# A list scheduler's table of step times, latencies and priorities, replaced as a whole, in a one-core attention, gated-FFN and cosine-FFN kernel

## The chip, the cores and the metric

The kernel runs on 1 core of one Trainium2 chip. The metric is the device time of the program in microseconds (us). The granted clock of TensorE was 0.999 of full speed over the profiled execution.

## The reference

All tensors are fp32. Attention over 4 batches × 8 heads, 576 tokens, head size 64, then two feed-forward layers over 2304 tokens × 512:

```python
scores = q @ k.T / sqrt(64)
scores = where(scores >= max(scores) - tau, scores, -1e9)
attn = exp(scores - max(scores)); attn /= sum(attn) + 1e-09
x = attn @ v                                  # 2304 x 512 over all heads
xn = x / sqrt(mean(x * x) + 1e-06) * rms_g
x = (silu(xn @ w_gate) * (xn @ w_val)) @ w_out   # 512 -> 1536 -> 512
h = x @ w_in                                  # 512 -> 2048
out = (h * cos(h)) @ w_out2                   # 2048 -> 512
```

## The kernel before

**Arithmetic.** A fp32 product is made of three matmuls on a high and a low part of each operand (`mm3`, L829 to L831; every `po`, `pc`, `px`, `pgv` of the layers is issued at L831). Both layers replace 8 block products by 7 (Strassen's way): products are called p1 to p7 and issued as p1, p2, p6, p5, p7, p4, p3. p1, p6, p7 and p4 follow each other in one PSUM bank, so between two of them an ACT copy of the bank (`rc` L1434 in layer 1, `rc2` L1721 in layer 2) or a DVE add must have read it. Weights arrive as 64-bit values and are converted on the chip (L398 to L416 during attention, L1061 to L1075 and others later).

**Stages**, in the time of the profiled execution: a head without much work on TensorE (0 to 8 us); attention to 283 us, 16 pairs of heads × 5 units of up to 128 queries × 2 heads; an early part of layer 1 (`pgv`, `px`; 283 to 331 us); the 7-product part of layer 1 (to about 722 us); layer 2, overlapped with the end of layer 1 from about 700 us on (to 1087.6 us); a tail of one add and the last output transfer.

**Attention.** A unit does scores `s` (L597), row maximum (L618, DVE), `exp` (L637, ACT), mask and row sum (L647, DVE), transposes `pst` on TensorE (L687) through a ring of three PSUM banks that ACT empties (`et<-pst`, L697), a remainder `psc` (L706 to L711, emptied by L715), and the product with v, `po` (L724: `av0`, `av1`), in one PSUM bank that ACT empties (`t<-po`, L734). Per pair the division (`div`, L741), squares (`sq`, L751) and their sum (`x_add`, L755) run on POOL; per batch a sum by matmuls with ones (`pss`, L764) and the root (L769, L775).

**What sets the order.** The kernel is written as steps. Each kind of step has a row in the table `STEPS`: its engine, its assumed time in ns, an offset to its place, and sometimes a landing time of its own (else that of its engine in `SIGNAL`). `Plan.order` (L208) simulates these times: again and again it takes the step that can start earliest, among equals the one of the smallest place, and puts it out. So the table decides the order of instructions on every engine, and nothing else of the program: the hardware waits on data at run time, whatever times the table holds. Steps of the kinds in `LOCK` share one simulated port of DVE and POOL, and a POOL step of the kinds in `BEHIND` gets a real dependence on the last such DVE step that was put out before it.

```python
        eng, ns, place, landing = (STEPS[kind] + (SIGNAL[STEPS[kind][0]],))[:4]
...
                    if best is None or (t, s["place"], n) < best:
                        best = t, s["place"], n
```

The place of a step is the offset plus 3500 (`UNIT`) times the unit of work that the program puts it at.

Of the kernel before, what the change touches and what calls it, by code (L numbers as in the profile page):

```python
# [25 lines left out]

UNIT = 3500
STEPS = {
    "xl3": ("SP", 2500, -17237051, 4000),
    "yl": ("SP", 3000, 1818983, 3000),  # L30
    "oc0": ("ACT", 620, -178776),
    "none": ("", 0, -8569405),
    "load_k": ("SP", 1700, -7132505, 5000),
    "load_q": ("SP", 2300, -18780962, 7000),
    "load_v": ("SP", 1700, 8049624, 5000),
    "pb": ("PE", 440, -91272),
    "pa": ("PE", 440, -8753194),
    "pc": ("PE", 355, 18191),
    "pb_a": ("ACT", 477, 288563),
    "pa_a": ("ACT", 580, 5964477),  # L40
    "pc_a": ("ACT", 362, -19061587),
    "pa_l": ("DVE", 605, -7927289),
    "pb_l": ("DVE", 605, -17590911),
    "pc_l": ("DVE", 470, -10454287),
    "s": ("PE", 885, -18879084),
    "s4": ("PE", 790, 9187294),
    "warm": ("PE", 640, 5100),
    "max": ("DVE", 680, -18861462),
    "exp": ("ACT", 675, 7067125),
    "th": ("POOL", 300, 3913872),  # L50
    "mask": ("DVE", 742, -235624),
    "t": ("PE", 445, 43347),
    "raw": ("ACT", 477, -526274),
    "c0": ("PE", 245, -944825),
    "c1": ("PE", 465, -9009928),
    "c_raw": ("ACT", 295, 1709382),
    "radd": ("POOL", 250, 4551371),
    "rinv": ("DVE", 375, 1620120),
    "r_out": ("SP", 2100, 9184652, 2500),
    "r_in": ("SP", 1700, 1717211, 11000),  # L60
    "av0": ("PE", 2212, -17630008),
    "av1": ("PE", 2745, -11610484),
    "avo": ("ACT", 300, 1749559),
    "div": ("POOL", 1385, 2473400),
    "xout": ("SP", 800, -8632135, 2500),
    "sq": ("POOL", 1122, 5175409),
    "x_add": ("POOL", 1385, 7064993),
    "xsum": ("PE", 1085, 828449),
    "mean": ("DVE", 140, -17859185),
    "rms": ("POOL", 1520, 12341),  # L70
    "rs_out": ("SP", 2500, -17590004, 2500),
    "x_load": ("SP", 600, -18407685, 4500),
    "x_p": ("POOL", 1010, 6936870),
    "x_a": ("ACT", 540, -160662),
    "x_d": ("DVE", 480, 5142752),
    "jdma": ("SP", 500, -587219, 5000),
    "j1": ("DVE", 440, 914524),
    "j2": ("DVE", 608, -18600102),
    "j_p": ("POOL", 1310, 11607829),
    "j_a": ("ACT", 540, -8610871),  # L80
    "gv": ("PE", 2090, 467903),
    "silu": ("ACT", 420, -17284285),
    "px": ("PE", 2090, -18876387),
    "pxc": ("ACT", 400, -7101975),
    "hmul": ("DVE", 480, -18857593),
    "hhi": ("ACT", 420, 1874630),
    "hlo": ("DVE", 480, -18400468),
    "gv_": ("PE", 2090, 1352763),
    "silu_": ("ACT", 420, -18407990),
    "px_": ("PE", 2090, 1742320),  # L90
    "pxc_": ("ACT", 400, 9160368),
    "hmul_": ("DVE", 480, 1821227),
    "hhi_": ("ACT", 420, -11626266),
    "hlo_": ("DVE", 480, -223025),
    "x_q": ("DVE", 480, -19287661),
    "x_a_": ("ACT", 540, 456116),
    "x_d_": ("DVE", 480, 2080948),
    "ld": ("SP", 1700, -16315, 2600),
    "st": ("SP", 1350, 994979, 2300),
    "re": ("SP", 1350, -18655029, 2300),  # L100
    "wj1": ("DVE", 420, 1306287),
    "wj2": ("DVE", 640, -18827972),
    "wm": ("ACT", 650, 7535685),
    "wp": ("POOL", 1310, 6985902),
    "ws": ("POOL", 720, -179615),
    "whi": ("ACT", 590, -38166),
    "wlo": ("DVE", 640, -19073380),
    "vhi": ("ACT", 370, 720),
    "vlo": ("DVE", 370, -9649757),
    "ty": ("DVE", 1700, 5179345),  # L110
    "tz": ("DVE", 480, 2119290),
    "tp": ("DVE", 880, -7385897),
    "thi": ("ACT", 830, 1707682),
    "tlo": ("DVE", 880, -186196),
    "tr": ("POOL", 1010, 779397),
    "tg": ("ACT", 480, 6985043),
    "pr": ("PE", 1050, 1271768),
    "p1": ("PE", 1050, 2576303),
    "rc": ("ACT", 470, 264284),
    "ra": ("DVE", 530, 3761292),  # L120
    "rs": ("ACT", 470, 43510),
    "rm": ("DVE", 500, -19406559),
    "rh": ("ACT", 480, 3025557),
    "rl": ("POOL", 1010, -18138630),
    "po": ("DVE", 900, 8219776),
    "pq": ("ACT", 800, 3470758),
    "wt": ("DVE", 350, 1371338),
    "ld2": ("SP", 1700, 4594862, 2600),
    "st2": ("SP", 1350, -151407, 2300),
    "re2": ("SP", 1350, 1749849, 2300),  # L130
    "wj12": ("DVE", 420, 1947299),
    "wj22": ("DVE", 640, -100554),
    "wm2": ("ACT", 650, 368993),
    "wp2": ("POOL", 1310, 7156916),
    "ws2": ("POOL", 720, 2588453),
    "whi2": ("ACT", 590, 287276),
    "wlo2": ("DVE", 640, 449005),
    "vhi2": ("ACT", 370, 984685),
    "vlo2": ("DVE", 370, 1294887),
    "tz2": ("DVE", 480, 2726933),  # L140
    "tp2": ("DVE", 880, -277554),
    "thi2": ("ACT", 830, -7727467),
    "tlo2": ("DVE", 880, 286304),
    "pr2": ("PE", 1050, 4791879),
    "oo": ("PE", 1390, 4793082),
    "tlp2": ("POOL", 1950, 2138257),
    "rc2": ("ACT", 470, -10651785),
    "ra2": ("DVE", 550, 2274412),
    "ct": ("ACT", 600, 2047040),
    "cf": ("DVE", 550, -18746959),  # L150
    "df": ("DVE", 530, 932632),
    "cb": ("ACT", 520, 4959718),
    "cs": ("ACT", 620, 1869941),
    "cg": ("DVE", 550, -7077025),
    "dg": ("DVE", 530, -11626296),
    "gh": ("ACT", 500, -179772),
    "gl": ("POOL", 1020, 2435746),
    "oe": ("DVE", 690, 5135108),
    "oc": ("ACT", 620, 1804210),
    "so": ("SP", 500, 4701633, 3000),  # L160
}
SIGNAL = {"PE": 190, "DVE": 110, "ACT": 145, "POOL": 60, "SP": 100, "": 0}
SWITCH = 100

LOCK = {
# [22 lines left out]
class Plan:  # L188
# [8 lines left out]
    def add(self, kind, at, fn, *args, after=(), take=(), free=()):  # L197
        eng, ns, place, landing = (STEPS[kind] + (SIGNAL[STEPS[kind][0]],))[:4]
        step = {
            "n": len(self.steps), "kind": kind, "at": at, "place": place + at * UNIT, "eng": eng, "ns": ns, "landing": landing,  # L200
            "fn": lambda: fn(*args), "after": [x for x in after if x], "take": take, "free": free,
        }
        for key in free:
            self.users[key] = self.users.get(key, 0) + 1
        self.steps.append(step)
        return step
# [87 lines left out]
def attention_moe_cos_kernel(  # L294
# [164 lines left out]
    nat, qk, un, hf, pr, xb, rm, sq, pre = {}, {}, {}, {}, {}, {}, {}, {}, {}  # L459
# [563 lines left out]
    def moe(plan, gm, g3, gvs, x1, x2_, x3, y3, pxc3):  # L1023

        add = plan.add
# [3 lines left out]
        def at(us):  # L1029
            return LATER + us / 3.5  # L1030
# [20 lines left out]
        raw, tmp, wd, lds = {}, {}, {}, []  # L1051
# [88 lines left out]
        for m, (g, prs) in enumerate(PASS):  # L1140
            fresh = m <= FIRST or not g
            save = m < FIRST
            for j in range(2):
                i = groups[g][1][j]
                t = due(m, j) - 26
                if fresh:
# [9 lines left out]
                    def op(o, a, b, fn):  # L1156
                        return lambda eng=pool if m else vec: eng.tensor_tensor(o(), a(), b(), op=fn)

                    def part(fn, a, b):
                        return lambda: fn(a, b)  # L1160

                    after = {tag: order[tag] and [] or [] for tag in order}
# [4 lines left out]
                    ws = "ws" if m else "wt"  # L1167
# [3 lines left out]
                    s4 = add(ws, at(t + 9), op(part(gate, 2, 4), part(gate, 2, 4), part(gate, 0, 2), SUB), after=[s2])  # L1171
# [4 lines left out]
                else:  # L1176
                    old, st = kept[g, j]
# [6 lines left out]
            for j in range(2):  # L1184
                i = groups[g][1][j]
                t = due(m, 1) + 12 + 3 * j - 24
# [6 lines left out]
                else:  # L1193
                    old, st = kept["out", g, j]
# [7 lines left out]
        y, z = {}, {}  # L1202
# [5 lines left out]
        def t_steps(pr):  # L1208

            c, c2 = pr  # L1210
            t = {0: -22, 2: 2, 4: BLOCK * first[pr] - 30}[c]
            ztag = "r" if not c else "hh"
            ttag = "ttb" if c == 2 else "tt"
            take = {cc: [("y", ("y", cc))] if cc != 5 else [] for cc in pr}
# [22 lines left out]
            ys = {}  # L1237
            for cc in pr:
# [4 lines left out]
                else:  # L1243
                    after = ys.get(c, [])[-1:] + XS[2, 3][1:]
# [9 lines left out]
            def z_sub(kk):  # L1254
                if not kk:
                    for n in range(2):
                        z[c, n] = late[ztag].tile([P, TC], F32, tag=ztag, name="z")
                vec.tensor_tensor(z[c, kk], y[c2][:, 2 + kk], y[c2][:, kk], op=SUB)

            zs = []  # L1260
            for kk in range(2):
                zs.append(add("tz", at(t + 1), lambda kk=kk: z_sub(kk), after=ys[c2] + zs, take=[(ztag, ("z", c, n)) for n in range(2)] if not kk else []))

            def psub(a, b, o):
                return lambda: vec.tensor_tensor(o(), a(), b(), op=SUB)
# [533 lines left out]
        t = t_l2  # L1799
# [315 lines left out]
```

## Time and profile before

| what | value |
|---|---|
| device time, 3 runs | 1095.17 us median (1093.99 to 1095.41) |
| the profiled execution: its own time / its span | 1093.68 us / 1091.9 us |
| instructions | 18813 |
| busy share PE, PE loads, DVE, ACT, POOL | 99%, 89%, 78%, 63%, 40% |
| chain that ended last | PE 96%, ACT 2%, DVE 1% |
| HBM | 139 GB/s over the span |

The span is the time on the core's engines in one profiled execution; the device time of that execution is 1.8 us longer. PE is the matmul part of TensorE and PEld its weight loads, which overlap. A bracket at a row's end is the engine's idle time before it and the instruction that ended it.

### The profile page before, as it was taken

Reading aid. Unit: us, or ns where it says so; the run is one execution under the profiler, and the core shown is the slowest. Engines: PE = TensorE matmul, PEld = TensorE weight load, DVE = VectorE, ACT = ScalarE, POOL = GpSimd, SP = SyncE. Lnnn points to the kernel's source line nnn. Section 1 sums busy time; section 2 is a strip of 40 time slices with the busy share of each in tenths; the row PEclk is TensorE's granted clock in tenths of the full one; section 3 lists DMA queues with packets and bytes.
Section 4 is the critical chain, followed back from the end, with each engine's and each line's share of the span. In section 5 each row is a group of like instructions: output and inputs, shape, how many; then the busy total and the mean of one; then the engine's idle time right before and its main releaser. Section 6 shows DMA issues by size and latency. Waiting matters only on the chain.

```text
span 1091.9 us, 18813 instructions
## 1 busy us (share of the span) xinstructions
PE 1079.7 (99%) x6720; PEld 975.5 (89%) x6720; DVE 854.0 (78%) x1683; ACT 692.5 (63%) x1316; POOL 432.5 (40%) x445
## 2 busy tenths in 40 slices
PE   8999999999999999999999999999999999999998
PEld 7777777777899999999999999988898889888887
DVE  7999999989689777586756653788888887865665
ACT  5888888888567554545545442587776666765553
POOL 1234244253532545655331441445455455222221
PEclk9999999999999999999999999999999999999999
DMA  5342443322635465643132576424544344274633
GB/s 133 90 132 80 117 121 99 102 67 60 190 98 204 153 214 192 198 171 110 59 95 80 167 264 225 165 70 143 184 176 153 131 169 145 53 256 145 195 104 97
DMA packets 113453, 152.97 MB, mean 140 GB/s; under 512 B 51632, under 2 KB 82128, under 8 KB 113360
## 3 DMA queue, kind: packets, MB, share of 16 engines
q1 hardware_dynamic: 112000, 151.31, 43.0%
q8 instruction: 53, 0.87, 0.4%
q10 hardware_dynamic: 1264, 0.43, 0.2%
q14 instruction: 40, 0.33, 0.1%
q0 software_dynamic: 96, 0.03, 0.0%
HBM read 103.16 MB, written 48.58 MB: 139 GB/s over the span
## 4 chain that ended last, share of the span: by engine, by line
PE 96%; ACT 2%; DVE 1%; DMA 0%; issue 0%; SPq 0%; ACTq 0%
PE pc L831 38%; PE po L831 18%; PE px L831 14%; PE po L724 8%; PE s L597 7%; PE pst L687 5%; PE pgv L831 3%; PE psc L706 1%; ACT et L697 1%; PE psa L518 0%; PE pss L764 0%; DMA k<-in_k_dram 0%; PE psb L518 0%; ACT e L637 0%; PE warm L796 0%
## 5 line engine op out<-in xcount | busy, mean ns | idle before, releaser
L831 PE MATMUL pc<-xh,w 128*128 128x384 f32 x896 | 257.1, 338 | 0.0
L831 PEld LDWEIGHTS pc<-xh,w 128*128 128x128 f32 x896 | 164.6, 188 | 2.2
L831 PE MATMUL pc<-xl,w 128*128 128x384 f32 x448 | 151.0, 337 | 0.0
L831 PE MATMUL pc<-th,w 128*128 128x384 f32 x448 | 132.8, 337 | 0.0
L1674 POOL TENSOR_TENSOR h<-hh,h 128x384 fp32r<-128x384 f32 x64 | 64.9, 1019 | 142.7 <-DVE hh L1657 48.7
L1075 POOL TENSOR_TENSOR wtmp<-wtmp,raw 128x512 int32<-128x512 int32 x68 | 89.2, 1320 | 75.5 <-DVE wtmp L1070 23.2
L1771 DVE TENSOR_TENSOR acc<-acc,po 128x512 f32<-128x512 f32 x126 | 85.1, 683 | 34.4 <-PE po L831 33.7
L1430 DVE TENSOR_TENSOR r<-r,pc 128x384 f32<-128x384 f32 x96 | 52.6, 550 | 74.6 <-ACT r L1434 54.5
L1434 ACT COPY r<-pc 128x384 f32<-128x384 f32 x96 | 45.9, 481 | 100.8 <-PE pc L831 100.5
L831 PE MATMUL po<-w,h 128*128 128x512 f32 x405 | 109.7, 396 | 0.0
L637 ACT ACTIVATE e<-s,m 128x576 f32<-128x576 f32 x128 | 95.9, 798 | 12.1 <-DVE s L618 11.9
L647 DVE SCALAR_TENSOR_TENSOR e<-s,th,e 128x576 f32<-128x576 f32 x128 | 102.2, 830 | 0.8 <-POOL th L628 0.7
L831 PE MATMUL px<-h,w 128*128 128x384 f32 x516 | 102.4, 338 | 0.0
L618 DVE TENSOR_SCALAR_CACHE_REDUCE s<-s 128x576 f32<-128x576 f32 x128 | 91.5, 752 | 5.8 <-PE s L597 5.5
L831 PEld LDWEIGHTS px<-h,w 128*128 128x128 f32 x516 | 91.7, 188 | 0.0
L831 PEld LDWEIGHTS po<-w,h 128*128 128x128 f32 x405 | 75.5, 188 | 14.0
L831 PEld LDWEIGHTS pc<-xl,w 128*128 128x128 f32 x448 | 84.2, 188 | 2.0
L1445 POOL TENSOR_TENSOR h<-q,h 128x384 fp32r<-128x384 f32 x43 | 44.2, 1033 | 101.9 <-DVE q L1473 40.1
L831 PEld LDWEIGHTS pc<-th,w 128*128 128x128 f32 x448 | 82.8, 188 | 1.7
L697 ACT COPY et<-pst 128x512 f32<-128x512 f32 x144 | 77.3, 604 | 8.3 <-PE pst L687 7.7
L831 PE MATMUL pc<-tl,w 128*128 128x384 f32 x224 | 75.6, 338 | 0.3 <-DVE tl L1572 0.3
L724 PE MATMUL po<-et,vn 128*64 128x320 f32 (+1 forms) x512 | 69.1, 412 | 1.4 <-ACT et L697 1.4
(194 smaller groups left out, 2653.6 us busy)
## 6 DMA issues: line engine op xcount, KB each, us to landing
wd<-w SPq DMA_DIRECT2D x67, 512.0 KB
w<-wd SPq DMA_DIRECT2D x53, 512.0 KB
raw<-in_moe_w_out_dram SPq DMA_DIRECT2D x30, 512.0 KB
raw<-in_moe_w_in_dram SPq DMA_DIRECT2D x16, 512.0 KB
raw<-in_moe_w_gate_dram SPq DMA_DIRECT2D x14, 512.0 KB
raw<-in_moe_w_val_dram SPq DMA_DIRECT2D x14, 512.0 KB
wq<-wd SPq DMA_DIRECT2D x14, 512.0 KB
x<-xb SPq DMA_DIRECT2D x16, 288.0 KB
```

The costliest lines, as they stand in the source:

```text
L597: nc.tensor.matmul(un[n]["ps", hd][:, c, 0:288], lhs, kh[bb][r, k0:k0 + 288], start=c not in [d for d, _ in todo[:x]], stop=c not in [d fo ...
L618: nc.vector.tensor_scalar(s.rearrange("p (c n) -> p c n", c=2), un[n].pop(("ps", hd))[:, :, 0:288], qscale[:, 0:1] if n % 5 == 4 else 1.0, ...
L637: nc.scalar.activation(un[n]["e"][:, hd], un[n]["s", hd], AF.Exp, bias=grp[group_of(n)]["m"][:, c], scale=-1.0)
L647: nc.vector.scalar_tensor_tensor(e, un[n].pop(("s", hd)), grp[group_of(n)]["th"][:, ci:ci + 1], e, op0=ALU.is_le, op1=ALU.mult, accum_out= ...
L687: nc.tensor.transpose(ps[:, c], e[:, hd, k0:k0 + P], ident)
L697: nc.scalar.copy(dst, src)
L724: nc.tensor.matmul(po[64 * hd:64 * hd + 64, :], vn[:, hd, c, :] if c < 4 else vl[:, hd, :], hf[j]["et"][:, hd, c, :] if c < 4 else hf[j][" ...
L831: nc.tensor.matmul(ps, w[a], x[bb], start=first and i == 0, stop=last and i == 2, skip_group_check=more)
L1075: pool.tensor_tensor(tmp[key], tmp[key], raw.pop(key)[:, :, :, 0], op=ADD)
L1430: return add("ra", at(t0 + when - 60), lambda: vec.tensor_tensor(tile_[o], tile_[o], ps[BANK[n]], op=ADD), after=after + [steps[n]], free= ...
L1674: hs2[x] = add("gl", at(t - 60), lambda: pool.tensor_tensor(H[x][1], g_tile[x], f(H[x][0]), op=SUB), after=[y], free=[("qq", x)])
L1771: vec.tensor_tensor(o, o, oacc.pop((c, q)), op=ADD)
```

## The change

All rows of `STEPS` get a new place offset, about 80 of them a new time and three (`rh`, `cs`, `gh`) a landing of their own; `SIGNAL` gets new latencies; and one kind of step, the subtraction `tz` (L1258) of the second and later pairs of blocks in layer 1, additionally waits for the first two steps `silu_`. No instruction is added or removed: each engine executes the same set as before (PE 6354, DVE 1397, ACT 1321, POOL 450, SP 577 rows in the program), in another order.

```diff
 STEPS = {
-    "oc0": ("ACT", 620, -178776),
+    "oc0": ("ACT", 482, 1004465),
...
-    "rc": ("ACT", 470, 264284),
+    "rc": ("ACT", 376, -10036888),
...
-SIGNAL = {"PE": 190, "DVE": 110, "ACT": 145, "POOL": 60, "SP": 100, "": 0}
+SIGNAL = {"PE": 200, "DVE": 114, "ACT": 138, "POOL": 55, "SP": 100, "": 0}
...
-                zs.append(add("tz", at(t + 1), lambda kk=kk: z_sub(kk), after=ys[c2] + zs, take=[(ztag, ("z", c, n)) for n in range(2)] if not kk else []))
+                zs.append(add("tz", at(t + 1), lambda kk=kk: z_sub(kk), after=ys[c2] + zs + ([s for s in plan.steps if s["kind"] == "silu_"][:2] if c else []), take=[(ztag, ("z", c, n)) for n in range(2)] if not kk else []))
```

The first 29 steps on PE and its last 8 stand as before. Three places show how the rest moves.

**Place 1: PE at the end of attention** (`pst` and `psc` are transposes, `po` with 64x256 is `av0` of the last unit pair, with 64x320 `av1`). Before:

```order
L687 MATMUL pst<-ident,e 128x128 x16
L724 MATMUL po<-et,vn 64x256 x8
L724 MATMUL po<-ec,v_101 64x256 x2
L706 MATMUL psc<-ident,e 128x128 x2
L710 MATMUL psc<-swap,el 128x128
L711 MATMUL psc<-ident,el 64x128
L687 MATMUL pst<-ident,el 128x128 x4
L724 MATMUL po<-et,vn 64x320 x8
L724 MATMUL po<-ec,v_101 64x320 x2
```

The change, on the same engine:

```order
L687 MATMUL pst<-ident,e 128x128 x12
L706 MATMUL psc<-ident,e 128x128 x2
L710 MATMUL psc<-swap,el 128x128
L711 MATMUL psc<-ident,el 64x128
L687 MATMUL pst<-ident,e 128x128 x4
L687 MATMUL pst<-ident,el 128x128 x4
L724 MATMUL po<-et,vn 64x256 x8
L724 MATMUL po<-ec,v_101 64x256 x2
L724 MATMUL po<-et,vn 64x320 x8
L724 MATMUL po<-ec,v_101 64x320 x2
```

The remainder and the last transposes now stand ahead of `av0`, and `av1` directly behind it.

**Place 2: PE in the early part of layer 1** (`pgv` is gate or value, `px` the product with w_out, `pss` the last sum of squares). Before, around `pss`:

```order
L831 MATMUL pgv<-xl,w 128x384
L831 MATMUL pgv<-xh,w 128x384 x2
L831 MATMUL pgv<-xl,w 128x384
L831 MATMUL pgv<-xh,w 128x384
L764 MATMUL pss<-ones,sq 128x1 x5
L831 MATMUL pgv<-xh,w 128x384
L831 MATMUL pgv<-xl,w 128x384
```

The change:

```order
L831 MATMUL pgv<-xl,w 128x384
L831 MATMUL pgv<-xh,w 128x384 x2
L831 MATMUL pgv<-xl,w 128x384
L831 MATMUL pgv<-xh,w 128x384
L764 MATMUL pss<-ones,sq 128x1 x5
L831 MATMUL px_4816<-hhi,w 128x384
L831 MATMUL px_4816<-hlo,w 128x384
L831 MATMUL px_4816<-hhi,w 128x384
```

`pss` moves from behind a `px` and a `pgv` group to ahead of that `px` group.

**Place 3: PE where layer 1 ends in layer 2** (`pc<-th,w` and the like are p7's last matmuls, `pc<-th,a` p4's first; six `po` with 128x512 are one output set of layer 2). Before:

```order
L831 MATMUL pc<-th,w 128x384
L831 MATMUL pc<-tl,w 128x384
L831 MATMUL pc<-th,w 128x384 x2
L831 MATMUL pc<-tl,w 128x384
L831 MATMUL pc<-th,w 128x384
L831 MATMUL pc<-th,a 128x384
L831 MATMUL pc<-tl,a 128x384
```

The change:

```order
L831 MATMUL pc<-th,w 128x384
L831 MATMUL pc<-tl,w 128x384
L831 MATMUL pc<-th,w 128x384 x2
L831 MATMUL pc<-tl,w 128x384
L831 MATMUL pc<-th,w 128x384
L831 MATMUL po<-w,h 128x512 x3
L831 MATMUL po<-w,hhi 128x512 x2
L831 MATMUL po<-w,hlo 128x512
L831 MATMUL pc<-th,a 128x384
L831 MATMUL pc<-tl,a 128x384
```

An output set now stands between p7 and p4.

## Rows read from the trace of the kernel before

**Rows 1.** The page, part 1: busy us (share of the span) xinstructions.

```profile
PE 1079.7 (99%) x6720; PEld 975.5 (89%) x6720; DVE 854.0 (78%) x1683; ACT 692.5 (63%) x1316; POOL 432.5 (40%) x445
```

**Rows 2.** The page, part 4: the chain that ended last, shares by engine.

```profile
PE 96%; ACT 2%; DVE 1%; DMA 0%; issue 0%; SPq 0%; ACTq 0%
```

**Rows 3.** Windows: stretch, us, busy us of PE, PEld, DVE, ACT, POOL, clock, DMA share, GB/s.

```profile
40.00:275.00 235.00, 234.11 (x2102) 179.02 (x2099) 224.34 (x602) 197.21 (x366) 91.86 (x102) 1.00 0.36 98
343.00:720.00 377.00, 377.00 (x2141) 376.21 (x2140) 260.38 (x402) 189.83 (x371) 160.42 (x158) 1.00 0.47 160
735.00:1076.00 341.00, 341.00 (x1689) 305.83 (x1688) 263.98 (x464) 223.06 (x426) 137.16 (x136) 1.00 0.45 153
```

**Rows 4.** Waits of PE: us in all, times, longest (first and last of seven).

```profile
PE po L724 <- ACT et L697: 1.4, 2, 0.8
...
PE pc L831 <- DVE tl L1572: 0.3, 1, 0.3
```

**Rows 5.** Timeline of PE, 34 to 42 us: start, us, engine, line, shape, [idle <-releaser].

```profile
34.72 1.15 PE L687 MATMUL pst<-ident,e 128*128 128x128 f32 x8 [0.37 <-ACT et L697]
...
39.72 2.37 PE L724 MATMUL po<-et,vn 128*64 128x320 f32 x16 [0.77 <-ACT et L697]
```

**Rows 6.** Timeline of PE, 269 to 282 us.

```profile
269.99 1.47 PE L687 MATMUL pst<-ident,e 128*128 128x128 f32 x12
...
274.23 2.04 PE L687 MATMUL pst<-ident,e 128*128 128x128 f32 x16
...
277.98 0.60 PE L724 MATMUL po<-ec,v 128*64 128x256 f32 x4
...
280.28 2.38 PE L724 MATMUL po<-et,vn 128*64 128x320 f32 x16 [0.67 <-ACT et L697]
```

**Rows 7.** Timeline of ACT, the copy that empties the bank of `av0`.

```profile
278.66 0.37 ACT L734 COPY t<-po 128x256 f32<-128x256 f32 x1 [1.62 <-PE po L724]
```

**Rows 8.** Timeline of PE, 304 to 313 us.

```profile
307.25 0.45 PE L831 MATMUL px<-hlo,w 128*128 128x384 f32 x1 [0.45 <-DVE hlo L866]
...
311.42 1.17 PE L764 MATMUL pss<-ones,sq 128*128 128x1 f32 x10
```

**Rows 9.** Timeline of POOL, 300 to 306 us.

```profile
300.54 1.45 POOL L741 TENSOR_TENSOR xb<-t,rb 128x576 f32<-128x576 f32 x1 [7.91 <-DVE xe L818]
302.84 1.15 POOL L751 TENSOR_TENSOR sq<-xb 128x576 f32<-128x576 f32 x1 [0.85 <-DVE xl L825]
304.55 1.43 POOL L755 TENSOR_TENSOR sq<-sq 128x576 f32<-128x576 f32 x1 [0.56 <-DVE xl L825]
```

**Rows 10.** Timeline of DVE, 295 to 300 us.

```profile
296.58 1.49 DVE L942 TENSOR_TENSOR acc<-acc,rs 128x384 f32<-128x384 f32 x3
...
299.86 0.55 DVE L818 TENSOR_TENSOR xe<-xe 128x384 f32<-128x384 f32 x1
```

**Rows 11.** Timelines of ACT and DVE: the second `silu_`, and the `tz` of the second pair.

```profile
319.12 0.47 ACT L854 ACTIVATE hh<-pgv 128x384 f32<-128x384 f32 x1
...
336.73 1.02 DVE L1258 TENSOR_TENSOR z<-acc 128x384 f32<-128x384 f32 x2
```

**Rows 12.** Timeline of PE, 721 to 727 us.

```profile
721.60 0.44 PE L831 MATMUL pc<-tl,w 128*128 128x384 f32 x1 [0.28 <-DVE tl L1572]
...
725.59 0.34 PE L831 MATMUL pc<-th,w 128*128 128x384 f32 x1
...
726.60 0.44 PE L831 MATMUL pc<-th,a 128*128 128x384 f32 x1 [0.67 <-ACT r L1721]
```

**Rows 13.** The chain near its end: start, us, engine, tile, line, instructions.

```profile
1070.14 1.40 PE po L831 x6
1071.53 1.06 PE pc L831 x6
```

**Rows 14.** The page, part 5: the copy after a product in layer 2.

```profile
L1721 ACT ACTIVATE r<-pc,quarter 128x384 f32<-128x384 f32 x72 | 41.5, 581 | 34.3 <-PE pc L831 33.4
```

**Rows 15.** Groups on DVE, 40 to 275 us: the second step of a weight conversion.

```profile
L403 DVE SCALAR_TENSOR_TENSOR wtmp<-raw,wtmp 128x512 int32<-128x512 int32 x5 | 3.5, 693 | 0.2
```

More of the change, by code (lines that the diff above doesn't have):

```diff
@@ L28 @@
 STEPS = {
-    "xl3": ("SP", 2500, -17237051, 4000),
-    "yl": ("SP", 3000, 1818983, 3000),
-    "oc0": ("ACT", 620, -178776),
[L32 to L118, printed above, removed]
-    "rc": ("ACT", 470, 264284),
[L120 to L160, printed above, removed]
+    "xl3": ("SP", 2500, -1701767, 4000),
+    "yl": ("SP", 3000, -11139283, 3000),
+    "oc0": ("ACT", 482, 1004465),
+    "none": ("", 0, -1876020),
+    "load_k": ("SP", 1700, -5527029, 5000),
+    "load_q": ("SP", 2300, -9482259, 7000),
+    "load_v": ("SP", 1700, 7416852, 5000),
+    "pb": ("PE", 440, -77239),
+    "pa": ("PE", 440, -5638801),
+    "pc": ("PE", 355, 11154),
@@ new lines @@
+    "pb_a": ("ACT", 467, -11435715),
+    "pa_a": ("ACT", 580, -11146563),
+    "pc_a": ("ACT", 360, -5882778),
+    "pa_l": ("DVE", 658, -7828259),
+    "pb_l": ("DVE", 603, -9058187),
+    "pc_l": ("DVE", 470, -8044940),
+    "s": ("PE", 884, -12393480),
+    "s4": ("PE", 790, -675299),
+    "warm": ("PE", 640, -1914122),
+    "max": ("DVE", 678, -3685963),
+    "exp": ("ACT", 668, -1611267),
+    "th": ("POOL", 300, -1364591),
+    "mask": ("DVE", 737, -2963797),
+    "t": ("PE", 437, 37596),
@@ new lines @@
+    "raw": ("ACT", 467, -3942240),
+    "c0": ("PE", 245, -191807),
+    "c1": ("PE", 465, -218755),
+    "c_raw": ("ACT", 264, -2933142),
+    "radd": ("POOL", 250, -1776241),
+    "rinv": ("DVE", 420, 4654631),
+    "r_out": ("SP", 2100, -1512300, 2500),
+    "r_in": ("SP", 1700, -1733440, 11000),
+    "av0": ("PE", 2214, -10841569),
+    "av1": ("PE", 2748, -1862531),
+    "avo": ("ACT", 345, 35246),
+    "div": ("POOL", 1391, 456711),
+    "xout": ("SP", 800, 6901600, 2500),
+    "sq": ("POOL", 1124, -1174650),
@@ new lines @@
+    "x_add": ("POOL", 1389, 7923289),
+    "xsum": ("PE", 1085, 4529846),
+    "mean": ("DVE", 110, -6206560),
+    "rms": ("POOL", 1520, -1683651),
+    "rs_out": ("SP", 2500, 7755832, 2500),
+    "x_load": ("SP", 600, -6210699, 4500),
+    "x_p": ("POOL", 980, 2276499),
+    "x_a": ("ACT", 507, -853426),
+    "x_d": ("DVE", 500, -1513694),
+    "jdma": ("SP", 500, -511120, 5000),
+    "j1": ("DVE", 416, -2243721),
+    "j2": ("DVE", 608, -8032087),
+    "j_p": ("POOL", 1290, -1444071),
+    "j_a": ("ACT", 509, -5604253),
@@ new lines @@
+    "gv": ("PE", 2090, 7537447),
+    "silu": ("ACT", 375, 82497),
+    "px": ("PE", 2115, -3457135),
+    "pxc": ("ACT", 371, 433645),
+    "hmul": ("DVE", 470, -3651752),
+    "hhi": ("ACT", 415, -1407870),
+    "hlo": ("DVE", 469, -1627361),
+    "gv_": ("PE", 2110, -8456382),
+    "silu_": ("ACT", 375, -3675507),
+    "px_": ("PE", 2115, -1458781),
+    "pxc_": ("ACT", 371, -10872633),
+    "hmul_": ("DVE", 466, -8036926),
+    "hhi_": ("ACT", 415, -5535415),
+    "hlo_": ("DVE", 469, -2991891),
@@ new lines @@
+    "x_q": ("DVE", 467, 7411401),
+    "x_a_": ("ACT", 500, -1335941),
+    "x_d_": ("DVE", 467, 462313),
+    "ld": ("SP", 1700, -1516972, 2600),
+    "st": ("SP", 1350, -6215911, 2300),
+    "re": ("SP", 1350, -8912306, 2300),
+    "wj1": ("DVE", 414, -11293188),
+    "wj2": ("DVE", 608, 1731797),
+    "wm": ("ACT", 571, 1788150),
+    "wp": ("POOL", 1275, 7563076),
+    "ws": ("POOL", 705, 1811208),
+    "whi": ("ACT", 521, -1178110),
+    "wlo": ("DVE", 602, -1454808),
+    "vhi": ("ACT", 298, 8501425),
@@ new lines @@
+    "vlo": ("DVE", 335, 372104),
+    "ty": ("DVE", 1667, -5923412),
+    "tz": ("DVE", 468, -7923433),
+    "tp": ("DVE", 868, 1783062),
+    "thi": ("ACT", 725, 4383646),
+    "tlo": ("DVE", 868, 7435888),
+    "tr": ("POOL", 972, -1762995),
+    "tg": ("ACT", 518, 13228),
+    "pr": ("PE", 1050, -2010806),
+    "p1": ("PE", 1050, -1939777),
+    "rc": ("ACT", 376, -10036888),
+    "ra": ("DVE", 466, 3750103),
+    "rs": ("ACT", 388, 4354444),
+    "rm": ("DVE", 469, -9559199),
+    "rh": ("ACT", 413, 4620433, 190),
@@ new lines @@
+    "rl": ("POOL", 972, -2353135),
+    "po": ("DVE", 865, 3725274),
+    "pq": ("ACT", 698, -2946700),
+    "wt": ("DVE", 343, -1502095),
+    "ld2": ("SP", 1700, 7407834, 2600),
+    "st2": ("SP", 1350, -4552783, 2300),
+    "re2": ("SP", 1350, -684450, 2300),
+    "wj12": ("DVE", 412, 4362029),
+    "wj22": ("DVE", 608, -8933785),
+    "wm2": ("ACT", 565, -2054504),
+    "wp2": ("POOL", 1275, 7593747),
+    "ws2": ("POOL", 702, -241193),
+    "whi2": ("ACT", 521, -4260944),
+    "wlo2": ("DVE", 601, -8681454),
@@ new lines @@
+    "vhi2": ("ACT", 307, -1529239),
+    "vlo2": ("DVE", 335, -1757558),
+    "tz2": ("DVE", 468, -4005886),
+    "tp2": ("DVE", 868, 273353),
+    "thi2": ("ACT", 724, -7767502),
+    "tlo2": ("DVE", 868, -8208346),
+    "pr2": ("PE", 1050, 4798303),
+    "oo": ("PE", 1393, 4800580),
+    "tlp2": ("POOL", 1805, 7637523),
+    "rc2": ("ACT", 476, -1749371),
+    "ra2": ("DVE", 466, 7420530),
+    "ct": ("ACT", 481, -1729320),
+    "cf": ("DVE", 470, -1788607),
+    "df": ("DVE", 468, 153586),
+    "cb": ("ACT", 512, -7167919),
@@ L161 @@
+    "cs": ("ACT", 463, -8041396, 95),
+    "cg": ("DVE", 468, -4002098),
+    "dg": ("DVE", 468, 64862),
+    "gh": ("ACT", 405, 3889283, 195),
+    "gl": ("POOL", 975, -1169137),
+    "oe": ("DVE", 600, -1780084),
+    "oc": ("ACT", 482, -7229980),
+    "so": ("SP", 500, -10489250, 3000),
 }
-SIGNAL = {"PE": 190, "DVE": 110, "ACT": 145, "POOL": 60, "SP": 100, "": 0}
+SIGNAL = {"PE": 200, "DVE": 114, "ACT": 138, "POOL": 55, "SP": 100, "": 0}
 SWITCH = 100
```

## The prediction
> **What bounds the kernel now.** I read the page's busy shares first, then its chain, then the windows by stage, and last the waits of PE and the timelines around each of them. The shares [rows 1] and the chain [rows 2] name one engine: PE is busy 99% of the span and makes 96% of the chain. The windows [rows 3] say where this holds: in the steady part of layer 1 PE is busy 377.00 of 377 us, in that of layer 2 341.00 of 341, in attention 234.11 of 235. Since the change adds and removes no matmul, it can only win what PE loses between them. The list of PE's waits after the head has seven rows, from 1.4 us to 0.3 [rows 4], some 3.8 us in all. So the stake is small, 0.35% of the time, and the question is which of these waits the new order removes and which it makes. Ahead of 27 us and in the last 8 steps PE's order is the same; nothing is to be won there.
>
> The sum goes against the profiled execution's own time, 1093.68 us; the median is 1.49 higher.
>
> **Term 1, 33 to 43 us.** Before, PE waits 0.37 us at 34.72 and 0.77 at 39.72 for the copy of a transposed tile [rows 5]. The new order puts the transposes of those units earlier among the scores, so that one of these waits, at least in part, has other matmuls over it. The ring has three banks and ACT is as slow as before, so I take −0.4; ends are 0 (the wait moves with the transposes) and −1.14 (both go).
>
> **Term 2, 279 to 280 us (place 1 of the order).** Before, the remainder and the last transposes stand between the two products with v, and the second waits 0.67 us for a copy of a transposed tile [rows 6]. Now they stand ahead of the first product, whose 2.5 us hide those copies. But the second product now stands right behind the first, and both use one bank: it must wait until ACT has copied the first out. The first ended at 277.98 + 0.60 = 278.58, the copy ran from 278.66 to 279.03 [rows 6, 7], so about 0.45 us of new wait stands against 0.67 of old: −0.2. Ends: 0 (ACT is behind with the transposes' copies) and −0.67.
>
> **Term 3, 306 us (place 2).** Before, `px` waits 0.45 us for the low part of its input, while the 1.17 us of the sum of squares `pss` come only at 311.42 [rows 8]. Now `pss` stands ahead of this `px` and covers the wait. That holds if the squares are ready: before, POOL sat idle 7.91 us, tied behind a DVE step at 299.86, and its three instructions ended at 304.55 + 1.43 = 305.98 [rows 9, 10]. In the new order the tie goes to a step that DVE starts at 296.58, 3.3 us earlier, so they end near 302.7 at the latest, and `pss` is wanted at about 304.3. I take −0.6: the shown 0.45, and about 0.15 by which the matmuls around it ran apart. Ends: −0.75, and +1.7 if the POOL steps stay where they are (305.98 against 304.3).
>
> **Term 4, 721 to 727 us (place 3).** Before, PE waits 0.28 us for the low part of an input and 0.67 before p4, because p4 stood right behind p7 in the same bank [rows 12]: from the start of p7's last matmul (725.59) to p4's (726.60) 1.01 us passed, 0.18 of which the matmul itself needs (1.06 us for six [rows 13]), so 0.84 is lost. Now an output set of six matmuls stands between them; one takes 1.40 us [rows 13], more than the 1.01, so the second wait goes. The first, with its ragged edges 0.45 by the starts, should go too, as the subtractions on DVE that feed it stand some steps earlier in the new order. What is late next is DVE's add ahead of p3: by the durations above it ends some 0.1 us before PE wants it. I take −1.4; ends: −1.6 (every start gap here), and −0.4 (the add is late, and one of the two waits comes back).
>
> **Term 5, the ring of transposes elsewhere.** Three transposes in a row took 1.47 us and four 2.04 [rows 6]; at the pace of the three, the four would take 1.47 × 4/3 = 1.96 or a little less, so a fourth in the ring's three banks costs about 0.1 us that no wait shows. In the order, a bank is used again within about 1 us 76 times of 240 before and 68 now; 8 × 0.05 = −0.4, as most of them have some slack. Against it, PE changes between the tile shapes of scores, products and transposes 137 times in place of 134, at about 0.1 each: +0.3. Together −0.1, with ends of ±1.0.
>
> **The layers' steady part, and the added wait: nothing.** All other matmuls of the layers stand in other places of the queue too, but PE waits for nothing there now [rows 3], and between two products of one bank the new order leaves never less than one other product, 1.06 us [rows 13]; that spacing occurs before, without a wait. The cover is thinner, though: see the fourth rival. The new wait of `tz` ends when the second `silu_` does, at 319.12 + 0.47 = 319.6, and the `tz` it applies to first ran at 336.73 [rows 11]: 17 us of cover. If that were gone, DVE and through it PE would be late by the difference.
>
> **Sum.** −0.4 − 0.2 − 0.6 − 1.4 − 0.1 = −2.7 us: 1091.0 for a profiled execution and 1092.5 at the median, −0.25%. A measurement of this kernel can tell about 0.2%, 2.2 us, from no change. Taken together, not all at one end, the bounds leave −5 to +0.5 of this case: 1090 to 1095.7.
>
> **Rivals.**
> *Given back in attention* (0.25). DVE is busy 224.34 of 235 us there [rows 3]; the new order leaves the last weight conversion to the end and puts its two steps of 0.69 us [rows 15], and one shorter of about 0.4, between the last masks. If these masks set the end of attention, PE loses 1.8 us. For it speaks how full DVE is; against it, that what stands later at the end stood earlier before, so the masks in between start sooner. Time: 1092.5 + 1.8 = 1094.3, no change that can be told.
> *More room in attention than the waits show* (0.10). The weight loads fill 376.21 of 377 us in layer 1 but only 179.02 of 235 in attention (76%) [rows 3]; and four transposes lost time without a wait on show [rows 6]. If the 0.1 us that a close use might cost (term 5) comes back at 50 of the 76, that is −5: 1087.5. The Trainium skill, page "Perfetto Trace Analysis", section "Identifying the Most-Contended Engine", says that matmul busy time is a bad measure because matmuls are pipelined, and that the share of weight loads tells more. By that rule attention would have a quarter of its time to give. The trace agrees only in part: layer 2's loads fill 305.83 of 341 (90%) where nothing waits, so the shapes of the matmuls set this share as well.
> *Reserve gone in layer 2: slower* (0.10). Between p1 and p6, which share a bank, 16 of the 24 blocks had one product and two output sets before, 1.06 + 2 × 1.40 = 3.86 us [rows 13]; now 14 have one product and one set, 2.46. The copy between them needs 1.01 in all when ACT is free [rows 12]. If ACT comes over 1.45 us late, p6 waits; at the seam such a hit showed 0.67 us [rows 12]. From 8 blocks on (8 × 0.67 = 5.4 against 2.7 + 2.2) the kernel is slower by over 0.2%; with all 14, +9.4 − 2.7: 1101.9. Against it: this copy's own group sat idle 34.3 us before its 72 runs, 33.4 of them waiting for PE [rows 14], so ACT is mostly there first.
> *The table changes too little.* The order differs on every engine, so this is no case of its own; if the new places only shuffle covered work, terms 1 to 3 are 0 and 1094 results, which lies in the first case's range.
>
> **How the numbers follow.** My forecast's case has 0.55, the rivals 0.25, 0.10 and 0.10. The range, 1089.6 to 1096.0, holds the forecast's and the first rival's cases with their bounds, and leaves out the two others, 0.2. Faster by over 0.2% (under 1093.0): four fifths of the forecast's case, 0.44, and the second rival, 0.10: 0.54. Within 0.2%: the rest, 0.11 + 0.25 = 0.36. Slower: 0.10.
>
> **What would show it.** Right: no wait of PE near 306 and none at 721 and 726; in place of the wait for a transposed tile at 280, one of about 0.45 for the copy L734; less than 1.1 us of waits between 33 and 43; the two steady windows of the layers still without idle time, with as many matmuls per us. Wrong: a wait of `pss` for POOL (term 3), a wait of p3 or p4 for DVE after 720 (term 4), DVE or ACT named before the products of layer 2 between 735 and 1076 (third rival), or a gap of PE behind the masks at 270 to 283 (first rival). If attention ends over 3 us earlier, the second rival holds.

## The result and the profile after

The changed kernel takes 1110.87 us (median of 5 runs, 1107.39 to 1111.7) against 1095.17 (5 runs, 1093.93 to 1095.61): a ratio of 1.0139, 95% interval 1.0121 to 1.0157. It is slower by 15.7 us where a gain of 2.7 was forecast, and the time lies far above the range. The profiled execution is the shortest of the five, 1107.39 us, so the trace accounts for 13.7 of the 15.7.

The page, part 1, of the changed kernel (busy us, share of the span, instructions), against [rows 1]:

```profile
PE 1086.9 (98%) x6720; PEld 974.2 (88%) x6720; DVE 874.8 (79%) x1683; ACT 692.4 (63%) x1316; POOL 444.5 (40%) x445
```

The instructions are the same in number, but DVE is busy 20.8 us longer and POOL 12.0. The windows of the three stages (columns as in [rows 3]):

```profile
40.00:275.00 235.00, 233.28 (x2095) 178.43 (x2095) 225.09 (x603) 197.65 (x364) 93.85 (x102) 1.00 0.38 102
343.00:720.00 377.00, 372.89 (x2101) 368.18 (x2100) 260.63 (x393) 187.35 (x367) 161.29 (x156) 1.00 0.47 160
735.00:1076.00 341.00, 337.73 (x1657) 299.16 (x1657) 275.39 (x459) 222.79 (x428) 147.02 (x143) 1.00 0.45 154
```

Attention does nearly the work of before in its 235 us. In the layers PE is no longer busy without a gap, and the count of matmuls tells the loss better than the busy time: layer 1 does 2101 in place of 2141 in 377 us, 40 fewer at 0.176 us, 7.0 us; layer 2 1657 in place of 1689, 32 fewer at 0.20, 6.5 us. These two make 13.5 of the 13.7. What PE waits for (us in all, times, longest; five of twelve rows):

```profile
PE pc L831 <- ACT r L1434: 3.2, 4, 1.8
PE pc L831 <- ACT r L1721: 2.9, 5, 0.6
...
PE po L724 <- ACT t L734: 0.6, 1, 0.6
PE pc L831 <- DVE r L1430: 0.6, 2, 0.4
PE po L724 <- ACT et L697: 0.5, 1, 0.5
```

The two rows on top are the copies of a product's bank: the one in layer 1 (L1434) is new, the one in layer 2 (L1721) had a single wait of 0.7 us before [rows 12] and now has five, at other places. The waits of the weight loads show more of the same loss than those of the matmuls:

```profile
PEld pc L831 <- ACT r L1434: 5.7, 8, 2.2
PEld pc L831 <- ACT r L1721: 4.8, 6, 1.0
...
PEld pc L831 <- DVE w L1113: 1.8, 5, 0.4
```

Together 12.3 us, where no such row of the layers exceeds 1.0 us in the kernel before. One of these places in layer 2, read backwards. The timelines of PE, ACT, POOL and DVE around 790 us (start, us, engine, line, shape, idle before and releaser):

```profile
793.84 0.45 PE L831 MATMUL pc<-th,a 128*128 128x384 f32 x1 [0.31 <-ACT r L1721]
```

```profile
789.63 0.56 ACT L1721 ACTIVATE r<-pc,quarter 128x384 f32<-128x384 f32 x1
790.82 1.16 ACT L1107 ACTIVATE w<-wtmp 128x512 fp32r<-128x512 f32 x2 [0.62 <-POOL wtmp L1075]
791.87 0.51 ACT L1654 ACTIVATE hh<-hh 128x384 f32<-128x384 f32 x1
792.29 0.62 ACT L1107 ACTIVATE w<-wtmp 128x512 fp32r<-128x512 f32 x1
792.81 0.49 ACT L1662 CAST hhi<-hh 128x384 fp32r<-128x384 f32 x1
793.21 1.04 ACT L1721 ACTIVATE r<-pc,quarter 128x384 f32<-128x384 f32 x2
```

```profile
788.18 1.02 POOL L1674 TENSOR_TENSOR h<-hh,h 128x384 fp32r<-128x384 f32 x1 [2.12 <-DVE wtmp L1070]
789.16 1.62 POOL L1075 TENSOR_TENSOR wtmp<-wtmp,raw 128x512 int32<-128x512 int32 x1
```

```profile
787.32 0.69 DVE L1070 SCALAR_TENSOR_TENSOR wtmp<-raw,wtmp 128x512 int32<-128x512 int32 x1
787.93 0.68 DVE L1771 TENSOR_TENSOR acc<-acc,po 128x512 f32<-128x512 f32 x1
...
789.83 1.37 DVE L1648 SCALAR_TENSOR_TENSOR hh<-hh,r 128x384 f32<-128x384 f32 x1 [0.21 <-ACT hh L1645]
```

PE waits for the copy at 793.21. The copy stands in ACT's queue behind five instructions (three L1107, L1654 and L1662); ahead of them ACT had been idle 0.62 us until POOL's conversion L1075 ended at 790.78. That conversion began at the end of POOL's step at 788.18, which is tied to the DVE step at 787.32. The next DVE step started at 787.93, so in the planner's count, where the step takes 608 ns, the port is free then; POOL started 0.25 us later. Over all tied POOL steps that found POOL idle and their data there, this hand-over is about 0.23 us in the middle in both kernels (some 140 steps in the one before, some 130 in the changed one). The plan has none: the next user of the port may start when the DVE step's time is over. At 789.83 the two engines also collide: a DVE step that takes 0.55 us elsewhere takes 1.37 while POOL's conversion runs, and the conversion takes 1.62 where its group's mean before was 1.32.

Why did the kernel before stand this? Its hand-overs are as long. But between instructions back to back the trace shows L1771 on DVE every 604 ns, the DVE steps L1648 every 469, the POOL step L1674 every 977 (medians): the new table has 600, 468 and 975, the old one 690, 530 and 1020. For these three groups the new times are right, and the old ones had 40 to 90 ns too much. Laid against the plan (each step's start in the trace minus its planned start, minus the same for PE), DVE, ACT and POOL of layer 2 (735 to 1076 us) ran ahead by 0.34, 0.24 and 0.27 us in the middle before; now they run behind by 0.27, 0.25 and 0.54, and one in ten by about 1.0 to 1.2. The plan has margins of fractions of a microsecond in layer 2, and they are gone. In layer 1 (343 to 720 us) there was less to lose: DVE and ACT led by 0.09 and 0.06 us in the middle and POOL trailed by 0.02; now all three trail, by 0.06, 0.04 and 0.39.

That is **theory 1**: the hand-over of the port that the plan lacks, for which the old times' surplus had paid. **Theory 2**: the new places stand the copies too late in ACT's queue, whatever POOL does. **Theory 3**: collisions at the port, which a looser tie makes worse.

### The profile page after: what moved, and what is told of

The parts are those of the page before. It is cut to its first block, busy times and chain, and to the rows that moved or that the text cites. A ratio compares the mean times of both kernels' runs of the same rounds, so it can differ in the third digit from the quotient of the medians.

```text
span 1105.6 us, 18818 instructions
## 1 busy us (share of the span) xinstructions
PE 1086.9 (98%) x6720; PEld 974.2 (88%) x6720; DVE 874.8 (79%) x1683; ACT 692.4 (63%) x1316; POOL 444.5 (40%) x445
## 4 chain that ended last, share of the span: by engine, by line
PE 66%; DVE 17%; ACT 7%; POOL 4%; DMA 3%; issue 2%; SPq 0%; POOLq 0%; ACTq 0%; DVEq 0%
PE pc L831 25%; PE po L831 12%; PE px L831 9%; PE po L724 6%; PE s L597 6%; PE pst L687 5%; DVE hh L1657 2%; DVE wtmp L1070 2%; DVE hh L1648 1%; DVE e L647 1%; POOL wtmp L1075 1%; ACT et L697 1%; DVE wtmp L1061 1%; POOL wtmp L1604 1%; DVE s L618 1%
## 5 line engine op out<-in xcount | busy, mean ns | idle before, releaser
L831 PE MATMUL pc<-xh,w 128*128 128x384 f32 x896 | 261.7, 339 | 1.2 <-DVE r L1430 0.6
L1075 POOL TENSOR_TENSOR wtmp<-wtmp,raw 128x512 int32<-128x512 int32 x68 | 91.2, 1345 | 98.8 <-DVE wtmp L1070 34.8
L1674 POOL TENSOR_TENSOR h<-hh,h 128x384 fp32r<-128x384 f32 x64 | 65.6, 1029 | 130.0 <-ACT h L1662 54.1
L1771 DVE TENSOR_TENSOR acc<-acc,po 128x512 f32<-128x512 f32 x126 | 85.8, 683 | 22.5 <-PE po L831 22.4
L1434 ACT COPY r<-pc 128x384 f32<-128x384 f32 x96 | 45.7, 478 | 85.3 <-PE pc L831 85.0
L618 DVE TENSOR_SCALAR_CACHE_REDUCE s<-s 128x576 f32<-128x576 f32 x128 | 91.5, 752 | 4.0 <-PE s L597 3.4
L831 PE MATMUL pc<-th,a 128*128 128x384 f32 x224 | 67.8, 343 | 4.0 <-ACT r L1721 2.9
```

Of the source, the lines that this page charges most:

```text
L618: nc.vector.tensor_scalar(s.rearrange("p (c n) -> p c n", c=2), un[n].pop(("ps", hd))[:, :, 0:288], qscale[:, 0:1] if n % 5 == 4 else 1.0, ...
L831: nc.tensor.matmul(ps, w[a], x[bb], start=first and i == 0, stop=last and i == 2, skip_group_check=more)
L1075: pool.tensor_tensor(tmp[key], tmp[key], raw.pop(key)[:, :, :, 0], op=ADD)
L1674: hs2[x] = add("gl", at(t - 60), lambda: pool.tensor_tensor(H[x][1], g_tile[x], f(H[x][0]), op=SUB), after=[y], free=[("qq", x)])
L1771: vec.tensor_tensor(o, o, oacc.pop((c, q)), op=ADD)
```

## The experiments

**The tie, one lock step earlier, in both orders.** No instruction moves in any queue; only the run-time tie of a POOL step goes to the DVE lock step before the one it had, so that POOL is ready at the port when that ends. Nothing but the port rests on this tie.

```diff
-        tiling, port, holder = 0, 0, None
+        tiling, port, holder, earlier = 0, 0, None, None
...
                 if eng == "DVE":
-                    holder = s
+                    earlier, holder = holder, s
                 elif s["kind"] in BEHIND:
-                    s["behind"] = holder
+                    s["behind"] = earlier
```

> The changed kernel with its order untouched; only the run-time tie of a POOL step goes to the DVE lock step before the one it had. Theory 1 (the new table's times are right one by one, but the hand-over of the shared port from DVE to POOL, some 0.2 us from the end of the DVE step in the planner's count to the POOL step's start, is not in the plan; the old times' surplus paid for it): the POOL steps start 0.2 us or more sooner and 10 us or more of the 15.7 lost come back: 1092 to 1101. Theory 2 (the new places put the ACT copies of the product banks too late in ACT's queue, whatever POOL does): no change, 1107 to 1112. Theory 3 (the ports collide more with a looser tie): slower than 1112.

> The kernel before with its order untouched and the same looser tie. Theory 1: its order has a surplus on DVE that already covers the hand-over, so little is won: 1091.5 to 1095.5. Theory 2: the same as before, 1094 to 1096. Theory 3: slower than 1097.

Measured: 1096.95 us in the changed order (ratio to the kernel before 1.0016, interval 1.0007 to 1.0026): 13.9 of the 15.7 us come back. In the order before: 1095.33 (1.0006, 0.9997 to 1.0016), no change. Theories 2 and 3 fall as the main cause by the first result; the second fits theory 1 and theory 2 alike. A looser tie could also win by letting POOL run ahead of the DVE step, but by the trace this is rare: behind 283 us 10 of 317 tied POOL steps start before the DVE step they had been tied to. The windows of the changed order with the earlier tie:

```profile
343.00:720.00 377.00, 374.17 (x2112) 372.36 (x2111) 259.26 (x393) 189.59 (x369) 176.53 (x157) 1.00 0.47 159
735.00:1076.00 341.00, 341.00 (x1689) 305.82 (x1688) 272.30 (x463) 222.23 (x427) 151.83 (x141) 1.00 0.46 155
```

Layer 2 does its 1689 matmuls again, without a gap. Layer 1 still does 29 fewer than before, 5.1 us, part of which the places at 306 us and 721 us (terms 3 and 4) give back.

**No tie at all.**

```diff
-            if s.get("behind"):
+            if s.get("behind") and False:
```

> The changed kernel with its order untouched and no tie of a POOL step to a DVE step at all. Theory 1: the hand-over is gone, but POOL now takes the port whenever its data are there and DVE's lock steps wait up to 1.3 us behind it: not better than the changed kernel, 1105 to 1125, with longer DVE steps (df, dg at L1655 and after) in the trace. Theory 2: 1107 to 1112, no change.

Measured: 1114.0 us (one run). Without a hand-over, but with the port to whoever comes first, DVE is busy 899.2 us (874.8 with the ties, 863.1 with the earlier ones). More of the time is now lost in attention, which does 2045 matmuls in its 235 us in place of 2095; the layers, with 2108 and 1662, do little better than with the ties (2101 and 1657). So leaving out the tie is no cure: POOL has to come behind the right DVE step, and without delay.

**Which stage: the two orders spliced.** Every prefix of one order is a valid start, so the rest can follow in the other's order. The ties are set anew by the joined order. Both kernels here are cut at 273 us of the planner's time, the end of attention (283 us in the trace).

```diff
+        first = self.order()
+        ...                      # the second table's times and places
+        second = self.order()
+        out = [s for s in first if s["first"] < CUT] + [s for s in second if s["first"] >= CUT]
```

> The changed order up to the end of attention (283 us), the order before from there on. Theory 1 and 2 alike (the loss lies in the layers, after 331 us): 1094 to 1097.5, that is within +1 of attention's own loss. If attention's new order is to blame for the late POOL and DVE in the layers: over 1103.

> The order before up to the end of attention (273 us of the planner's time), the changed order with its own ties from there on: the complement of the run with the two parts the other way round. If the loss lies in the layers' order alone: 1105 to 1111. If it needs the attention's order as well: under 1101.

Measured: 1095.69 us (1.001, 1.0001 to 1.002) with the changed attention alone, 1108.51 (one run) with the changed layers alone. The loss is the layers', and the new attention costs about 0.7 us.

**Twice the hand-over in the kernel before.** A small POOL instruction ahead of each tied POOL step takes the tie; as control the same one stands behind it.

```diff
             n = len(done)
+            if s.get("behind"):
+                tc.nc.gpsimd.tensor_scalar(Plan.scratch, Plan.scratch, 1.0, None, op0=ALU.add)
             s["fn"]()
...                          # and the scratch tile, set to 0 once
```

> The kernel before, order and ties untouched; in front of each tied POOL step one more small POOL instruction (an add on a 128x8 scratch tile, about 0.27 us), which takes the tie, so each hand-over of the port from DVE to POOL is about twice as long. Theory 1 (the hand-over is what the order cannot stand): the surplus of the old times is used up and TensorE waits appear in the layers, 1099 to 1115. Theory 2 (places): the order is as before and POOL is 40% busy, 1094 to 1097.

> Control for the run with the small POOL instruction ahead: the same instruction behind each tied POOL step, so POOL has the same work but the hand-over is as before. Theory 1: 1094 to 1099, less than half of the other's loss. If mere POOL work is what hurts: the same as the other.

Measured: 1117.55 us ahead, 1104.56 behind (one run each). The small instruction puts the tied step behind it off by 0.20 us in the middle, so the hand-over nearly doubles. Both times lie above what was expected, and the control shows that POOL's work as such is not free here: 9.8 us, presumably since the next tied step of a busy POOL comes late as well. The 13.0 us between the two are the price of the later start. PE's largest waits in the layers are for the copies and the add of a product's bank, as in the changed kernel, though no step of the order has moved; the control has them too, but smaller (2.4 and 1.2 us for the two copies). The last two rows are waits that the kernel before has as well, 0.3 and 0.4 us there (five of the longest waits; the edit shifts lines by 3):

```profile
PE pc L834 <- ACT r L1437: 5.0, 6, 1.6
PE pc L834 <- ACT r L1724: 3.8, 5, 1.1
PE pc L834 <- DVE r L1433: 2.4, 3, 1.0
...
PE pc L834 <- DVE tl L1575: 1.4, 1, 1.4
PE px L834 <- DVE hlo L869: 1.4, 1, 1.4
```

**The rest, at 459 us.** With the earlier tie one wait of 1.8 us for the copy L1434 stayed, at 459.94 us. In the changed kernel it stands at 464.82; there the timelines of PE, POOL and SP read:

```profile
464.82 0.44 PE L831 MATMUL pc<-th,w 128*128 128x384 f32 x1 [1.85 <-ACT r L1434]
```

```profile
459.36 4.53 POOL L1232 TENSOR_TENSOR acc<-acc,rs 128x384 f32<-128x384 f32 x4 [2.33 <-DMA acc<-x]
```

```profile
450.17 0.34 SPq L1049 DMA_DIRECT2D wd<-w  x1
450.56 0.43 SPq L1049 DMA_DIRECT2D rs<-rs  x1
451.04 0.80 SPq L1049 DMA_DIRECT2D acc<-x  x1
```

ACT scales layer 1's next input (L1235) ahead of that copy; the scalings wait for POOL, and POOL for a load that was issued at 451.04 behind a store of weights and used 8.3 us later, where the plan has 6.0 (3000 + 3000 ns, as before). Two repairs of the order by hand, both with the earlier tie: the first puts three scalings behind the copy, the second the load ahead of that store, where the order before has it.

```diff
...
+        late = [s for s in order if s["n"] in (2528, 2530, 2532)]
+        order = [s for s in order if s not in late]
+        i = [s["n"] for s in order].index(2278) + 1
+        order[i:i] = late
...
```

```diff
...
+        load = [s for s in order if s["n"] == 2526]
+        order = [s for s in order if s["n"] != 2526]
+        i = [s["n"] for s in order].index(1761) + 1
+        order[i:i] = load
...
```

> The changed order with the earlier tie, and three scalings of layer 1's input on ACT (L1235, which wait for POOL and through it for a load) moved behind the copy of a product bank (L1434) that TensorE awaits at about 459 us. If what is left of the loss there (a wait of 1.8 us) is this place in ACT's queue: 1.5 to 2 us less than without the move, 1094.5 to 1096. If the late load alone sets it: no change.

> The changed order with the earlier tie, and the load of one input block of layer 1 (the first of the two for which POOL waited 3.2 us at 454 us) put ahead of a weight store in SP's queue, where the order before has it; it is issued some 5 us sooner. If the late load is what holds POOL's and ACT's queues there: the wait of 1.8 us of TensorE for the copy L1434 goes, 1.5 to 2.5 us less than with the earlier tie alone, 1094.4 to 1095.5. If ACT's queue alone sets it: no change, 1096.5 to 1097.5.

Measured: 1097.26 us (1.002, 1.0011 to 1.0029) for the copy first, no gain. The wait of 1.8 us is gone, but the next copy stands behind the next scaling, which still waits for POOL (lines shifted by 5):

```profile
464.94 0.62 ACT L1240 ACTIVATE acc<-acc,g_sb 128x384 f32<-128x384 f32 x1 [0.26 <-POOL acc L1237]
465.46 0.46 ACT L1439 COPY r<-pc 128x384 f32<-128x384 f32 x1
```

PE waits 1.32 us for it at 465.97, and 1.60 us for another copy at 654.07, which was not followed up. The load earlier: 1094.98 (0.9999, 0.999 to 1.0009), 2.0 us less than the earlier tie alone. Its POOL row has no wait for the load any more, and layer 1 does 2133 matmuls:

```profile
451.36 2.95 POOL L1237 TENSOR_TENSOR acc<-acc,rs 128x384 f32<-128x384 f32 x3
```

```profile
343.00:720.00 377.00, 375.85 (x2133) 374.50 (x2132) 261.79 (x398) 191.17 (x373) 177.22 (x158) 1.00 0.47 159
```

So the earlier tie (13.9) and one load (2.0) come to the 15.7 in sum. Not every loss is gone: layer 1 does 8 matmuls fewer than before (1.4 us) and the new attention costs its 0.7, which the gains at 306 and 721 us balance.

**New times under old places.** The table's times and latencies from the change, its places from before.

> The table with the places of before, but the new times and latencies. If places fit only the times that they were searched with (and the new times leave the hand-over no surplus): clearly slower than the changed kernel, 1115 to 1145. If the new times alone were harmless and the new places at fault: 1094 to 1098.

Measured: 1132.07 us (one run; its attention window has a granted clock of 0.98, the other runs 1.00, so a part of its loss there may be the clock's). The queues come out differently from both kernels. It says that the old places do not go with the new times; it does not tell theory 1 from others.

**The better parts together.** From 640 us of the planner's time the changed order with the earlier tie, before it the order of before; then the same with the changed order in the first 45 us too.

> The order before with its ties up to 640 us of the planner's time, from there the changed order with the earlier tie. It has the seam of the change (term 4, -1.3 by the trace) and no loss in layer 2 if theory 1 holds: 1092.8 to 1094.8. If the earlier tie only helps together with the changed order of layer 1: over 1097.

> As the order before up to 640 us and the changed order with the earlier tie behind it, but with the changed order also up to 45 us of the planner's time, where the trace of the change shows one wait of TensorE less (0.77 us, term 1). If the gains add: 1092.3 to 1093.6. If the splice costs a new wait: over 1094.

Measured: 1093.38 us (0.9985, 0.9976 to 0.9994) and 1091.83 (0.9977, 0.9967 to 0.9986). The second, a little below its expected range, beats both kernels, by 0.23% the one before. Its layers have no gap:

```profile
343.00:720.00 377.00, 377.00 (x2144) 376.66 (x2143) 261.76 (x404) 191.82 (x374) 161.79 (x157) 1.00 0.46 157
735.00:1076.00 341.00, 341.00 (x1690) 306.24 (x1688) 272.64 (x465) 221.80 (x425) 149.56 (x139) 1.00 0.46 154
```

## Why the prediction was wrong, step by step

The forecast's terms at the five places, in the changed kernel's timeline of PE (first scores, 35 us, end of attention, 306 us):

```profile
8.30 0.77 PE L597 MATMUL s<-khi,qhi 64*128 64x288 f32 x4 [0.50 <-ACT qhi L550]
...
35.03 1.15 PE L687 MATMUL pst<-ident,e 128*128 128x128 f32 x8 [0.37 <-ACT et L697]
...
281.15 2.37 PE L724 MATMUL po<-et,vn 128*64 128x320 f32 x16 [0.55 <-ACT t L734]
...
283.99 0.44 PE L831 MATMUL pgv<-xh,w 128*128 128x384 f32 x1
...
305.14 1.17 PE L764 MATMUL pss<-ones,sq 128*128 128x1 f32 x10
...
308.21 0.33 PE L831 MATMUL px<-hhi,w 128*128 128x384 f32 x1
308.76 0.44 PE L831 MATMUL px<-hhi,w 128*128 128x384 f32 x1 [0.22 <-ACT hhi L862]
309.35 0.44 PE L831 MATMUL px<-hlo,w 128*128 128x384 f32 x1
```

- **Term 1** (−0.4): right and a little larger; of the two waits [rows 5] one is left, the 0.77 is gone.
- **Term 2** (−0.2): right. The wait for the transposes' copy went, and the new one for the single bank (L734) took its place, 0.55 against 0.67 [rows 6].
- **Term 3** (−0.6): failed. The squares came in time: `pss` ran at 305.14 without a wait. But ACT's high part now comes late as well: the starts from 308.21 to 309.35 take 1.14 us where two matmuls take 0.36, 0.8 lost, about as much as the 0.6 of before. The gain is there with the earlier tie, whose trace has no wait at this place: counted by the matmuls done, it wins 0.7 us between 300 and 313 us.
- **Term 4** (−1.4): right. PE has no wait between 720 and 760 us; counted by the matmuls done, the change wins 1.3 us from 700 to 760 us.
- **Term 5** (−0.1): mis-sized, by more than its bound. From the first score to the first `pgv` PE takes 283.99 − 8.30 = 275.7 us; before it was 275.2 (this row of before, from its timeline, and its first score at 7.96):

```profile
283.13 0.44 PE L831 MATMUL pgv<-xh,w 128*128 128x384 f32 x1
```

  With 0.9 won by terms 1 and 2, the rest of attention lost some 1.4 us; the bound was 1.0. Two new waits of the scores for DVE's row maximum (L618) show 0.5 of it; the rest stays open.
- **"The layers' steady part, and the added wait: nothing"** is the step that failed, by 13.5 us. It looked at PE's own order: one product between two of a bank, a spacing that occurs before without a wait. Whether the copy is in time was taken from how punctual ACT had been, not from what ACT waits for: its queue hangs on POOL's conversions, and POOL's on the DVE step that holds the port. All three queues were reordered to tighter times. The added wait of `tz` itself was rightly put at nothing: with the old table no queue of any engine changes by it, and in the changed kernel's trace the `tz` ran at 332.18 us, 11 us behind the end of the second `silu_` (320.34 + 0.48).
- **The third rival** ("reserve gone in layer 2") had the mechanism, ACT's copy late for the next product of a bank, and the right sign, at a chance of 0.10 and 1101.9 us. It looked for it at p1 and p6; it struck ahead of p4 (793.84 above, and four more blocks behind it), and in layer 1 too. Its counter-evidence, that this copy's group waited 33.4 of 34.3 us for PE [rows 14], was a sum over all 72: it does not tell how close the nearest one is.
- **The first rival** (a wait behind the last masks) did not come. **The second**, beside which stood the Trainium skill's page "Perfetto Trace Analysis", section "Identifying the Most-Contended Engine", did not either: attention's weight loads fill 178.43 of 235 us, 179.02 before, and the change won no time there. In one thing the page's warning on matmul busy time fits these runs: PE is busy 98% of the span after the change and 99% before, and it is the loads' waits and the counts of matmuls that show the loss.

What is shown: that the tied starts of POOL lose the time (the earlier tie in the changed order; the small instruction ahead and behind), that they cost layer 2 all of its 6.5 us, and that one load costs 2.0. That the old times' surplus is what carried the hand-over before is argued from the table and the engines' lead over the plan in layer 2, and in layer 1 that lead was small; neither the old times under the new places nor a table with the new times, the hand-over in the plan and places searched for both was tried.

## What to carry to other kernels

A plan with exact times for every step and none for what lies between two engines has less margin than one with round, too long times; before a table is tightened, lay the trace against the plan and see which engine runs behind it. Priorities chosen against a model can spend whatever slack the model shows, so the model needs the waits that the chip adds (here the port's hand-over and the landing of loads) before they are chosen. Where PE is fully busy, judge a new order by the engine furthest behind the copies that PE needs, and by the latest of them, not by their mean.

## What the runs showed of the hardware

- POOL starts about 0.23 us (middle of some 140 steps) after the point at which DVE itself goes on to its next instruction, when it waits for that DVE step. With a tie to an earlier step it issues sooner and then stands at the port: the mean of L1674 (`h<-hh,h`, 343 to 1076 us) rises from 1030 ns to 1103, and the kernel is 13.9 us faster.
- A DVE step that met a running POOL step took 1.37 us in place of 0.55 and ended 0.42 us behind POOL's step (791.20 against 790.78). In layer 2 the group L1648 (`hh<-hh,r`) averaged 564 ns before, 776 in the changed kernel, 702 with the earlier tie; the same step with its second input in PSUM (`hh<-hh,pc`) took 553, 550 and 550. By the Trainium skill, page "SBUF — State Buffer", section "SBUF: two separate sides", the port pair that the two engines share is an exclusive lock that one instruction holds to its end; the row at 789.83 agrees.
- A load of an input block (`acc<-x`) was used 8.3 us after its issue, the plan's 6.0 being the same in both tables.
